# Chunk-selecting attention into a gMLP block: a new table of orders, engines and PSUM banks

## The chip, the cores and the metric

The kernel runs on one core of one Trainium2 chip. The metric is the device time of one execution in microseconds (us); the median of three runs stands for a kernel. In the text PE is TensorE, DVE VectorE, ACT ScalarE, POOL GpSimd and SP the queue of SyncE, which issues DMAs.

## The reference

The first half is attention over q, k and v of 4 batches, 8 heads, 768 rows and 64 columns, where each row of q looks only at 6 of the 24 chunks of 32 keys: those whose upper bound is highest. The second half is a gMLP block on the attention's output, with weights of 512 to 1024, a gating matrix over the 768 rows, and 512 to 512 back.

```
k_min, k_max = k_chunks.min(axis=3), k_chunks.max(axis=3)
ub = sum(maximum(q*k_min, q*k_max), axis=-1)          # 24 bounds for each row
ub = where(causal, ub, -1e9); top_chunks = argsort(ub)[..., -6:]
scores = where(in a top chunk and not in the future, q @ k.T / 8, -1e9)
x = softmax(scores) @ v                                # then heads side by side: 4 x 768 x 512
h = gelu_tanh(x @ w_in); u, v = h[..., :512], h[..., 512:]
v_n = (v - mean(v)) / sqrt(var(v) + 1e-6) * g_ln
out = x + (u * (w_sg @ v_n + b_sg)) @ w_out
```

## The kernel before

The work is cut into 16 pairs of heads (p = 0 to 15; four pairs make one batch) and 4 gMLP blocks (b = 0 to 3, one for each batch). For a pair, `kside` (L561) transposes the keys on PE ("ktr"), reduces each chunk to its minimum and maximum on DVE (L570, into `Wall`), and copies the transposed keys out of PSUM into `KA` ("kev", L364 or L367). From pair 10 on `kside_full` (L585) casts the keys ("kcast", into kbx or IND) and lets a DMA transpose them into `KA`. `qside` (L628) transposes the queries, copies them into `qT` ("qev"), makes their positive part `rT` ("rel"), and casts them into `QA` ("qcast"); `vside` casts the values into `vx` ("vcast"). `select` (pairs 0 to 3, L651) and `select_full` (two pairs at once, L704) compute the bounds on PE, transpose them on DVE into `U`, take the eight largest of each row with MAX8, compare (`Dn`) and transpose back (`Dt`). For pairs 4 to 15 `Dt` is then copied into rows of `QA` ("qd"), so that one matmul gives the score and its mask. `scores` and `scores_full` (L804, L768) run the score matmuls into the two PSC banks, ACT takes exponentials (L844, L795) into `E`, POOL clears the part in the future (L800, "aff"). `head` (L855) multiplies with the values ("pv", L867; "pvd", L874), DVE takes the reciprocal of the sum (L882, "rcp"), and the product goes into `XS` ("xs"): one DVE instruction for six tiles (L890), or six on ACT (L888).

When a batch is complete, `xtrans` brings `XS` transposed into `xT` (by PE and an eviction "xev" for block 0 and the last piece, else by DMA, "dt_x"), and `moe_h` (L912) runs its matmuls: "hv" (L921) with a GELU on ACT (L925), statistics on DVE, the normalised `vhat` (L944 on ACT, else on DVE, "vhat"), and "hu" (L961) with its GELU. `moe_g` (L970) multiplies with the gating matrix `wsgT` (L978), scales and gates on DVE (L984, L988), multiplies with w_out (L997), adds x (L1007) and stores (L1014, "st"). The last block's second half is stored in halves of 256 columns, out of `qn`. Early on the weights are cast to bf16 ("wic", "wsc", "woc"), w_sg is transposed by PE and evicted into `wsgT` ("wev"), and the masks `IND` and `INDF` are made ("ini", L410; "mrow" copies INDF into `KA`).

None of this is issued in the order of the program. `_build` (L259) only records operations with `Program.op` (L57): engine, function, a cost in ns, a tag, what is read and written. `TABLE` (L1093) says in which order each of the five queues issues them, which PSUM bank each of 328 tiles takes ("slots"), and for some movable operations which engine ("engine"); an operation that is not named there takes the first engine in its call of `flex` (L356) or `either` (L373). `place` (L101) adds the dependence of a PSUM tile on the one before it in its bank, `link` (L123) puts a wait wherever an operation depends on another queue, and `emit` writes the queues out. A queue issues strictly in its order, so an instruction that waits holds all behind it. The costs were used in the search that made the table; nothing at run time reads them.

`flex` is the helper through which nearly all copies, casts and relus go; its last lines choose the instruction:

```
        eng = ENG.get("_".join(str(x) for x in tag), first)

        def fn(e):
            if eng == "act":
                return e.activation(dst(), src(), ACTF.Relu if relu else ACTF.Copy)
            if relu:
                return e.tensor_scalar(dst(), src(), 0.0, None, op0=ALU.max)
            return e.tensor_copy(dst(), src())
```

So an ACT copy is L364, a relu on DVE or POOL is L366, a copy on these L367.

## Time and profile before

| | us |
|---|---|
| median of three runs (lowest, highest) | 214.52 (213.18, 215.04) |
| span of the profiled execution | 211.8 |
| the profiled execution's own time | not shown with the profile; the median is 2.7 above the span |
| busy: PE, DVE, ACT, POOL | 198.9, 182.5, 168.0, 125.5 |
| granted clock of TensorE | 1.00 of full speed in every stretch |

The span runs from the first instruction to the last. An engine's busy time counts its own instructions; PE's is modelled from pipelined matmuls, so that it can read a little high. The chain of waits follows the work that ended last back to the start. The stretches below are cut where the first hv matmul of blocks 0, 1 and 2 starts (42.2, 101.3 and 150.5) and at three points between and behind them.

### The profile page before, as it was taken

How to read it: one execution, taken by the hardware profiler on the slowest of the kernel's cores; microseconds unless marked ns; L12 is line 12 of the kernel's file. 1: busy time of each engine (PE TensorE's matmuls, PEld its weight loads, DVE VectorE, ACT ScalarE, POOL GpSimd, SP SyncE). 2: the span in 40 equal slices, each digit the busy share in tenths (PEclk: the TensorE clock that was granted, in tenths of full speed). 3: DMA queues.
4: the chain of work that ended last, by engine and by line, in shares of the span. 5: the costliest groups of instructions: out<-in, count | busy, mean ns of one | idle time of the engine just before them, and what ended most of it. 6: DMA issues, size and time to landing. Idle time of an engine off the chain costs nothing.

```text
span 211.8 us, 6001 instructions
## 1 busy us (share of the span) xinstructions
PE 198.9 (94%) x2347; PEld 128.0 (60%) x2363; DVE 182.5 (86%) x526; ACT 168.0 (79%) x271; POOL 125.5 (59%) x170
## 2 busy tenths in 40 slices
PE   7788999999999998989999989999999999999993
PEld 2556777845675676668356766676545767555641
DVE  3899899799999998889999997868977786687994
ACT  3678999999999999999779968999878979258000
POOL 7648997883849997969843977399370163011000
PEclk9999999999999999999999999999999999999999
DMA  7999999996399989998899386399990004301217
GB/s 152 219 220 231 232 256 324 335 292 125 92 213 272 216 156 235 190 180 148 176 256 203 65 196 120 87 235 168 216 233 0 3 3 138 88 0 56 92 50 248
DMA packets 99773, 35.58 MB, mean 168 GB/s; under 512 B 94497, under 2 KB 95265, under 8 KB 99746
## 3 DMA queue, kind: packets, MB, share of 16 engines
q1 hardware_dynamic: 99746, 35.21, 78.7%
q8 instruction: 18, 0.29, 0.6%
q14 instruction: 9, 0.07, 0.1%
HBM read 24.38 MB, written 6.29 MB: 145 GB/s over the span
## 4 chain that ended last, share of the span: by engine, by line
PE 59%; ACT 20%; DVE 14%; DMA 4%; issue 2%; SPq 0%; DVEq 0%
PE PSG L978 11%; ACT E L795 10%; PE PSC L789 9%; PE PSG L961 8%; PE PSG L997 8%; PE PSG L921 7%; PE PSG L867 5%; DVE Wall L570 4%; PE PSG L540 3%; ACT XS L888 3%; DMA KA<-kbx 2%; PE PSC L829 2%; PE PSG L874 2%; DMA kn<-in_k_dram 2%; DVE KA L367 1%
## 5 line engine op out<-in xcount | busy, mean ns | idle before, releaser
L795 ACT ACTIVATE E<-PSC 128x1024 bf16<-128x1024 f32 (+1 forms) x72 | 62.8, 925 | 3.4 <-PE PSC L789 2.8
L789 PE MATMUL PSC<-QA,KA 128*128 128x128 bf16 (+2 forms) x336 | 37.7, 247 | 2.3 <-ACT E L795 2.0
L978 PE MATMUL PSG<-wsgT,vhat 128*128 128x384 bf16 x192 | 35.1, 327 | 0.1
L789 PEld LDWEIGHTS PSC<-QA,KA 128*128 128x128 bf16 x336 | 24.0, 98 | 13.8 <-ACT E L795 6.0
L800 POOL TENSOR_SCALAR_AFFINE_SELECT E<-E 128x768 bf16<-128x768 bf16 x24 | 20.5, 861 | 19.3 <-ACT E L795 19.0
L978 PEld LDWEIGHTS PSG<-wsgT,vhat 128*128 128x128 bf16 x192 | 17.7, 98 | 11.5 <-ACT XS L888 0.6
L367 POOL CAST QA<-qT 64x768 bf16<-64x768 f32 (+1 forms) x27 | 22.2, 821 | 4.0 <-PE PSC L789 2.4
L961 PE MATMUL PSG<-xT,winb 128*128 128x384 bf16 x128 | 23.9, 327 | 0.0
L570 DVE TENSOR_REDUCE Wall<-PSG 128x12 f32<-128x384 f32 x40 | 20.5, 547 | 2.8 <-PE PSG L540 2.8
L844 ACT ACTIVATE E<-PSC 128x1024 bf16<-128x1024 f32 (+1 forms) x24 | 20.7, 924 | 2.8 <-PE PSC L835 2.6
L966 ACT ACTIVATE uT<-PSG 128x384 bf16<-128x384 f32 x32 | 15.3, 487 | 8.4 <-PE PSG L961 8.1
L997 PE MATMUL PSG<-woutb,uT 128*128 128x512 bf16 x85 | 21.3, 379 | 0.6
L921 PE MATMUL PSG<-winb,xT 128*128 128x512 bf16 x91 | 21.1, 380 | 0.7 <-issue 0.4
L984 DVE SCALAR_TENSOR_TENSOR PSG<-PSG,glnT,bsgbc 128x384 f32<-128x384 f32 x32 | 19.5, 613 | 2.2 <-PE PSG L978 2.0
L367 POOL COPY QA<-Dt 32x576 bf16<-32x576 bf16 x19 | 12.5, 659 | 13.9 <-DVE Dt L748 9.7
L867 PE MATMUL PSG<-vx,E 128*128 128x65 bf16 x480 | 19.9, 194 | 0.7 <-ACT XS L888 0.5
L925 ACT ACTIVATE vgb<-PSG 128x512 f32<-128x512 f32 x24 | 14.0, 596 | 8.1 <-PE PSG L921 8.1
L867 PEld LDWEIGHTS PSG<-vx,E 128*128 128x128 bf16 x480 | 17.3, 97 | 3.5 <-ACT XS L888 1.4
L988 DVE TENSOR_TENSOR uT<-PSG,uT 128x384 bf16<-128x384 f32 x32 | 17.7, 554 | 0.9 <-ACT uT L966 0.2
L930 DVE BATCH_NORM_STATS2 stats<-vgb 128x6 f32<-128x512 f32 x24 | 15.8, 682 | 1.6 <-ACT vgb L925 1.4
L1007 DVE TENSOR_TENSOR osb<-PSG,XS 128x512 f32<-128x512 f32 x21 | 14.2, 683 | 3.4 <-PE PSG L997 3.0
L961 PEld LDWEIGHTS PSG<-xT,winb 128*128 128x128 bf16 x128 | 11.6, 98 | 8.8 <-ACT uT L966 2.3
(121 smaller groups left out, 388.8 us busy)
## 6 DMA issues: line engine op xcount, KB each, us to landing
...
```

What stands on the lines that cost most here:

```text
L367: return e.tensor_copy(dst(), src())
L570: P.op("dve", lambda d, m=m, op=op, t=t, c0=c0, c1=c1: d.tensor_reduce(W[w][:, m, c0 // 32:c1 // 32], t.ap()[:, 0:c1 - c0].rearrange("p (c ...
L789: r = e.matmul(t.ap()[:, o:o + n], KA[w][i][:, 128 * kb:128 * kb + 128], QA[w][i][:, q0:q0 + n], start=True, stop=True)
L795: P.op("act", lambda e, t=t, c0=c0, c1=c1, i=i: e.activation(E[es][:, i, c0:c1], t.ap()[:, 0:c1 - c0], ACTF.Exp, scale=SCALE), act(c1 - c0 ...
L800: P.op("pool", lambda g, ev=ev: g.affine_select(ev, ev, pattern=[[0, NT], [1, 128]], compare_op=ALU.is_ge, fill=0.0, base=0, channel_multi ...
L844: P.op("act", lambda e, t=t, c0=c0, c1=c1, n=n: e.activation(E[es][:, :, c0:c1], t.ap().rearrange("p (i x) -> p i x", i=2)[:, :, 0:n], ACT ...
L867: r = e.matmul(t.ap()[:, 65 * qb:65 * qb + 65], E[es][:, i, a:a + 128], vx[w][:, kb, i, :], start=first, stop=False, skip_group_check=True)
L921: r = e.matmul(t.ap()[:, 0:F], xT[s][:, dk, 128 * qt:128 * qt + 128], winb[:, dk, F:DFF], start=(dk == 0), stop=(dk == NDK - 1))
L961: r = e.matmul(t.ap()[:, 0:TG], winb[:, dk, 128 * fb:128 * fb + 128], xT[s][:, dk, TG * tg:TG * tg + TG], start=(dk == 0), stop=(dk == NDK ...
L978: r = e.matmul(t.ap()[:, 0:TG], vhat[s][:, sb, 128 * fb:128 * fb + 128], wsgT[:, sb, TG * tg:TG * tg + TG], start=(sb == 0), stop=(sb == N ...
L984: P.op("dve", lambda d, t=t, fb=fb, tg=tg: d.scalar_tensor_tensor(t.ap()[:, 0:TG], t.ap()[:, 0:TG], glnT[:, fb:fb + 1], bsgbc[:, TG * tg:T ...
L997: r = e.matmul(t.ap()[:, 0:DM], gT[s][:, fb, 128 * qt:128 * qt + 128], woutb[:, fb, :], start=(fb == 0), stop=(fb == NF - 1))
```

## The change

The table is replaced as a whole, and the cost functions take other constants. Both programs have 1293 operations with the same tags and shapes. 114 of the 328 PSUM tiles take another bank. 70 operations change engine: 22 from ACT to DVE, 18 from POOL to ACT, 13 from DVE to ACT, 10 from ACT to POOL, 4 stores from SP to ACT, 2 from POOL to DVE, 1 from DVE to POOL:

- ACT to DVE: rel_0, kev_1_0, kev_2_1, wev_2, wev_5, kev_3_0, qev_4_0, qev_4_1, rel_4, xev_0_0, xev_0_1, qev_5_0, rel_5, vhat_0_1, vhat_1_1, vhat_3_5, xs_4_0, xs_5_0, xs_9_0, xs_9_1, qev_14_1, qev_15_0
- POOL to ACT: ini_0, ini_1, qcast_0, wic_2, wsc_3, mrow_0_1_0, mrow_2_0_0, rel_7, rel_8, rel_12, rel_13, qd_9_1, kcast_12_0, kcast_15_0, qcast_13_1, qcast_14_0, qcast_14_1, vcast_14
- DVE to ACT: rel_1, rel_14, qev_2_0, qev_2_1, qev_5_1, qev_11_1, wev_3, kev_4_0_1, kev_4_1_0, kev_4_1_1, xev_0_2, vhat_0_3, vhat_3_1
- ACT to POOL: ini_2, wic_0, wsc_2, wsc_4, woc_2, vcast_4, qd_12_1, qd_13_0, qd_15_1, kcast_15_1
- POOL to DVE: rel_2, rel_15; DVE to POOL: qd_15_0; SP to ACT: the stores st_3_1, st_3_3_0, st_3_4_0, st_3_5_256

The diff, cut: the head of the SP order, the head of the engine list, and of the cost functions one, with the two lines of `flex` that set costs and the mark of a port.

```diff
-def dve(n, over=70, rate=1.0):
+def dve(n, over=64, rate=1.0):
     o = n / rate / 0.96 + over
-    return o, o + 83
+    return o, o + 84
...
-    def flex(first, others, dst, src, n, tag, reads, writes, ps=(), relu=False, shift=False):
+    def flex(first, others, dst, src, n, tag, reads, writes, ps=(), relu=False, shift=False, half=False):
...
-                 port=eng == "pool" or (eng == "dve" and relu))
+                 port=not ps)
...
     "sp": (
-        "38 36 37 39 41 40 43 42 45 46 74 47 73 48 72 71 136 142 44 134 135 133 183 49 79 184 132 138 82 80 185 75 186 "
+        "37 36 39 38 40 41 42 43 45 46 47 72 73 48 71 74 142 44 134 136 135 138 133 49 79 132 184 75 183 77 242 243 80 "
...
     "engine": (
-        "ini_0:pool ini_1:pool kev_0_0:dve rel_0:act wic_0:act kev_2_0:dve qev_2_0:dve qev_2_1:dve rel_2:pool "
+        "qcast_0:act rel_1:act rel_3:act wic_2:act mrow_3_0_0:act mrow_2_0_0:act mrow_0_1_0:act wsc_3:act rel_6:act "
...
```

In the SP order 36 and 37 are the two key loads of pair 0, 38 and 39 its two query loads. Lines of the changed kernel are two higher than those of the kernel before (L366 there is L364 here).

DVE in the opening, from the end of pair 0's selection to the transposing of pair 1's, before (a number behind a name is the buffer: rT1 is the positive part of pair 1's queries, U1, m8_1, Dn1 and Dt1 its selection, KA2 the keys of pair 2):

```order
L700 STREAM_TRANSPOSE Dt0<-Dn0 128x288
L582 TENSOR_TENSOR Wall<-Wall 128x24
L410 TENSOR_TENSOR INDF<-IND 128x768
L366 TENSOR_SCALAR rT1<-qT1 128x576
L367 CAST KA2_0<-PSG0 128x384
L570 TENSOR_REDUCE Wall<-PSG0 128x12 x2
L683 STREAM_TRANSPOSE U1<-PSG1 128x288
L690 MAX m8_1<-U1 128x8 x9
L570 TENSOR_REDUCE Wall<-PSG0 128x12
L367 COPY qT2<-PSG1 128x384 x2
L696 TENSOR_TENSOR Dn1<-U1,m8_1 128x288
L700 STREAM_TRANSPOSE Dt1<-Dn1 128x288
```

and after the change, the rows that end with the same instruction:

```order
L369 CAST KA1_0<-PSG0 128x384
L572 TENSOR_REDUCE Wall<-PSG0 128x12
L572 TENSOR_REDUCE Wall<-PSG1 128x12
L685 STREAM_TRANSPOSE U1<-PSG1 128x288
L369 CAST KA2_0<-PSG0 128x384
L692 MAX m8_1<-U1 128x8 x9
L572 TENSOR_REDUCE Wall<-PSG0 128x12
L698 TENSOR_TENSOR Dn1<-U1,m8_1 128x288
L584 TENSOR_TENSOR Wall<-Wall 128x24
L368 TENSOR_SCALAR rT2<-qT2 128x576
L412 TENSOR_TENSOR INDF<-IND 128x768
L702 STREAM_TRANSPOSE Dt1<-Dn1 128x288
```

The relu of pair 1 and the two copies of pair 2's queries have left for ACT; the cast of pair 1's keys and the relu of pair 2 have come. The INDF sum has moved from the front of the piece to a place between Dn1 and Dt1.

ACT at pairs 6 and 7, the last exponentials ahead of pair 5's XS copies, before:

```order
L364 ACTIVATE KA0_1<-PSG0 64x384
L795 ACTIVATE E0<-PSC0 128x640
L364 ACTIVATE KA1_0<-PSG0 64x384
L364 ACTIVATE KA1_1<-PSG0 64x384
L795 ACTIVATE E0<-PSC1 128x1024
L795 ACTIVATE E1<-PSC0 128x1024
L888 ACTIVATE XS<-PSG1,rden0 128x64 x6
L795 ACTIVATE E1<-PSC1 128x1024
L795 ACTIVATE E0<-PSC0 128x1024
L888 ACTIVATE XS<-PSG1,rden1 128x64 x6
```

and after (XS of six tiles is one head's product on ACT):

```order
L366 ACTIVATE KA0_0<-PSG0 64x384
L797 ACTIVATE E0<-PSC1 128x640
L366 ACTIVATE KA1_0<-PSG0 64x384
L366 ACTIVATE KA0_1<-PSG0 64x384
L366 ACTIVATE KA1_1<-PSG0 64x384
L797 ACTIVATE E1<-PSC1 128x1024
L797 ACTIVATE E0<-PSC0 128x1024
L797 ACTIVATE E1<-PSC1 128x640
L890 ACTIVATE XS<-PSG1,rden1 128x64 x6
```

Of the two groups of XS copies one is left here; the other is an instruction of DVE now.

ACT while pairs 9 to 11 are scored, before:

```order
L364 ACTIVATE kbx0<-kn2 128x6x64
L795 ACTIVATE E0<-PSC1 128x1024
L795 ACTIVATE E0<-PSC0 128x640
L888 ACTIVATE XS<-PSG1,rden1 128x64 x6
L364 ACTIVATE QA3_0<-Dt3 32x576
L795 ACTIVATE E0<-PSC0 128x640
L795 ACTIVATE E0<-PSC1 128x1024
L888 ACTIVATE XS<-PSG1,rden0 128x64 x6
```

and after:

```order
L366 ACTIVATE rT1<-qT1 128x576
L366 ACTIVATE QA3_0<-Dt3 32x576
L797 ACTIVATE E0<-PSC1 128x1024
L366 ACTIVATE QA1_1<-qT1 64x768
L797 ACTIVATE E0<-PSC0 128x1024
L366 ACTIVATE QA2_1<-qT2 64x768
L797 ACTIVATE E0<-PSC1 128x640
L797 ACTIVATE E0<-PSC0 128x1024
L797 ACTIVATE E0<-PSC1 128x1024
L366 ACTIVATE QA2_0<-qT2 64x768
```

The kbx cast (it comes 16 rows further down now) and both groups of XS copies are gone from this piece; a relu (rT1) and three casts of queries (QA1, QA2) stand between the exponentials instead.

## Rows read from the trace of the kernel before

**Rows 1.** The page, parts 1 and 4: busy time by engine, and the chain by engine

```profile
PE 198.9 (94%) x2347; PEld 128.0 (60%) x2363; DVE 182.5 (86%) x526; ACT 168.0 (79%) x271; POOL 125.5 (59%) x170
...
PE 59%; ACT 20%; DVE 14%; DMA 4%; issue 2%; SPq 0%; DVEq 0%
```

**Rows 2.** Each engine's busy time by stretch (us from the span's start, length first)

```profile
core 0: us, PE busy (x) PEld busy (x) DVE busy (x) ACT busy (x) POOL busy (x), PEclk, DMA share, GB/s
0.00:42.20 42.20, 37.68 (x605) 26.15 (x605) 36.18 (x119) 33.76 (x49) 33.01 (x54) 1.00 1.10 246
42.20:78.30 36.10, 35.27 (x320) 22.63 (x322) 35.40 (x108) 34.61 (x59) 26.88 (x36) 1.00 0.93 202
78.30:101.30 23.00, 21.10 (x366) 15.26 (x366) 20.19 (x60) 22.68 (x47) 19.27 (x25) 1.00 1.04 177
101.30:120.90 19.60, 19.55 (x134) 11.45 (x131) 18.97 (x56) 17.07 (x27) 12.64 (x17) 1.00 0.99 185
120.90:150.50 29.60, 28.18 (x490) 19.85 (x491) 24.48 (x78) 26.40 (x44) 21.38 (x26) 1.00 0.81 153
150.50:181.90 31.40, 31.00 (x311) 19.08 (x314) 24.50 (x62) 24.43 (x33) 10.98 (x14) 1.00 0.45 106
```

**Rows 3.** The chain of waits in order of time: start, us, what

```profile
1.88 3.56 DMA kn<-in_k_dram
...
6.07 1.95 DVE Wall L570 x4
...
58.30 0.81 ACT vhat L944
...
69.55 0.73 ACT vx L364
...
79.33 1.24 ACT XS L888 x6
...
121.12 4.56 DMA KA<-kbx
```

**Rows 4.** The timeline of SP's queue (start, us; in brackets idle time and what ended it)

```profile
1.31 1.11 SPq L510 DMA_DIRECT2D kn<-in_k_dram  x2
```

**Rows 5.** The timeline of PE at the start

```profile
1.24 3.95 PE L385 MATMUL PSC<-vhat 128*128 128x512 bf16 x9 [1.24 <-DVE vhat L379]
...
5.49 0.87 PE L540 MATMUL PSG<-identF,kn 128*128 128x128 f32 x6 [0.30 <-DMA kn<-in_k_dram]
```

**Rows 6.** Groups by line and shape: xcount | busy us, mean ns of one | idle before

```profile
L367 DVE CAST KA<-PSG 128x384 bf16<-128x384 f32 x3 | 1.6, 550 | 0.0
...
L890 DVE TENSOR_TENSOR XS<-PSG,rden 128x384 bf16<-128x384 f32 x27 | 14.8, 554 | 0.7
...
L364 ACT ACTIVATE rT<-qT 128x576 f32<-128x576 f32 x6 | 4.1, 690 | 0.0
...
L364 ACT ACTIVATE qT<-PSG 128x384 f32<-128x384 f32 x26 | 12.3, 491 | 1.6 <-PE PSG L540 1.3
...
L944 ACT ACTIVATE vhat<-vgb,nmr,rstd 128x512 bf16<-128x512 f32 x7 | 5.6, 809 | 0.5 <-DVE nmr L938 0.4
...
L367 POOL CAST QA<-qT 64x768 bf16<-64x768 f32 x23 | 18.9, 821 | 3.8 <-PE PSC L789 2.4 <-DVE qT L367 0.6 <-ACT E L795 0.2
```

**Rows 7.** The timeline of ACT while pairs 8 to 13 are made

```profile
125.70 0.52 ACT L364 ACTIVATE kbx<-kn 128x384 bf16<-128x384 f32 x1 [1.12 <-DMA KA<-kbx]
...
128.72 1.34 ACT L888 ACTIVATE XS<-PSG,rden 128x64 bf16<-128x64 f32 x6 [0.99 <-DVE rden L882]
```

**Rows 8.** The timelines of SP and DVE at the end

```profile
206.95 2.83 SPq L1014 DMA_DIRECT2D out_dram<-qn  x6
...
206.50 2.48 DVE L1007 TENSOR_TENSOR qn<-PSG,XS 128x256 f32<-128x256 f32 x6
```

**Rows 9.** The timeline of DVE, the subtraction of L624 at two times

```profile
95.94 0.17 DVE L624 TENSOR_TENSOR Wall<-Wall 128x48 f32<-128x48 f32 x1
...
143.10 1.32 DVE L624 TENSOR_TENSOR Wall<-Wall 128x48 f32<-128x48 f32 x1
```

More of the change, by code (lines that the diff above doesn't have):

```diff
@@ L227, in _, with gps, pe, dmac @@
                 run("sp", eng)
-def dve(n, over=70, rate=1.0):
+def dve(n, over=64, rate=1.0):
     o = n / rate / 0.96 + over
-    return o, o + 83
+    return o, o + 84
 def act(n):
-    o = n / 1.2 + 67
-    return o, o + 100
-def gps(n, over=45, rate=1.0):
+    o = n / 1.2 + 56
+    return o, o + 112
+def gps(n, over=47, rate=1.0):
     o = n / rate + over
-    return o, o + 50
-def pe(*cols, over=3):
-    o = sum(max(c / 2.4 + 2.5, 29) for c in cols) + over
-    return o, o + 164 - over
+    return o, o + 46
+def pe(*cols, over=0):
+    o = sum(max(c / 2.4 + 2.5, 30) for c in cols) + over
+    return o, o + 164
 def pe32(*cols):
-    o = sum(c * 2 / 2.4 + 2.5 for c in cols) + 28
-    return o, o + 136
-def dmac(issue=530):
+    o = sum(c * 2 / 2.4 + 2.5 for c in cols)
+    return o, o + 165
+def dmac(issue=450):
     return issue, issue
@@ L354, in _build @@
     ENG = dict(x.split(":") for x in TABLE["engine"].split())
-    def flex(first, others, dst, src, n, tag, reads, writes, ps=(), relu=False, shift=False):
-        costs = {"act": (n / 1.2 + 52, n / 1.2 + 168), "pool": (2.85 * n, 2.85 * n + 50) if relu else (n + 12 + 145 * shift, n + 60 + 160 * shift),
-                 "dve": (n / 1.92 + 67, n / 1.92 + 150) if relu else (n / 0.96 + 64, n / 0.96 + 147)}
+    def flex(first, others, dst, src, n, tag, reads, writes, ps=(), relu=False, shift=False, half=False):
+        rate = 0.96 if ps and not half else 1.92 if ps or not half else 3.84
+        costs = {"act": (n / 1.2 + 54, n / 1.2 + 170) if ps else (n / 1.2 + (210 if shift else 94), n / 1.2 + 204),
+                 "pool": (2.78 * n, 2.78 * n + 48) if relu else (n + 8 + 130 * shift, n + 54 + 10 * shift),
+                 "dve": (n / rate + 66 + 106 * shift, n / rate + 150)}
         eng = ENG.get("_".join(str(x) for x in tag), first)
@@ L374, in either @@
         eng = ENG.get("_".join(str(x) for x in tag), first)
-        o = P.op(eng, fns[eng], costs[eng], tag, reads=reads, writes=writes, ps=ps, port=eng == "pool" or (eng == "dve" and port))
+        o = P.op(eng, fns[eng], costs[eng], tag, reads=reads, writes=writes, ps=ps, port=port)
         o.alts = {x: costs[x] for x in (first,) + others}
@@ L522, in load_rows @@
             bass.AP(src.tensor, 2 * p * S * DH, ap)), dmac(),
-             (nm, p), writes=[(nm, s, i) for i in range(2)], dma=f"{nm}{s}", xfer={1: 1780, 2: 1350, NT: 1100}[run], bulk=NBULK)
+             (nm, p), writes=[(nm, s, i) for i in range(2)], dma=f"{nm}{s}", xfer={1: (1780, 96), 2: (1350, 48), NT: (1100, 16)}[run], bulk=NBULK)
     def load_v(p):
```

86 lines of the change are left out of this document (43 added, 43 removed), and 117 rows, old and new, of the table TABLE.

## Prediction

> **What bounds the kernel now.** I read the page's busy shares and chain of waits first: PE is busy 94% of a span of 211.8 us, and the chain that ended last lies on PE for 59%, on ACT for 20%, on DVE for 14% and on DMA for 4% [rows 1]. An order can take nothing from PE's own work, so whatever a new order gains comes out of the other 40%, and a table of stretches is needed that says where these lie. I cut the span at the starts of the gMLP blocks [rows 2]. PE is busy 37.68 of 42.20 us in the opening, 35.27 of 36.10 and 21.10 of 23.00 around block 0, 19.55 of 19.60 behind it, 28.18 of 29.60 while pairs 8 to 13 are made, 31.00 of 31.40 in the next. So two of the six stretches are full of matmuls, and PE's idle time in the others is 4.52, 0.83, 1.90 and 1.42 us. DVE comes closest beside it from 42.20 to 78.30 (35.40 of 36.10), ACT from 78.30 to 101.30 (22.68 of 23.00).
>
> The chain of waits says the same in single steps [rows 3]. In the opening it runs over the key load and then over DVE (reductions over key chunks, transposes, casts). From 58.30 on it is on ACT: a vhat of 0.81, later a vcast of 0.73 (vx), then XS copies of 1.24 us. At 121.12 it waits 4.56 us for a transposing DMA that ACT's kbx copy needs.
>
> **The change, part by part.** No operation comes or goes; 70 of 1293 stand on another engine, and the rest is order and PSUM banks. The cost functions feed nothing that is issued: 0. I price the stretches one at a time, against the profiled execution. Its own total is not shown beside its span; the median of the runs, 214.5, is 2.7 above the span, and I take these 2.7 us as what lies around it.
>
> *Opening, 0 to 42.2.* Both key loads of pair 0 now stand ahead of its query loads. Before, the two key issues take 1.11 us from 1.31 [rows 4], behind one query issue; the key rows need 3.56 us to land [rows 3], and the first transposes start at 5.49 with 0.30 of idle time that this load ended, because the warm-up matmuls were over at 1.24 + 3.95 = 5.19 [rows 5]. One issue earlier the load is in before the warm-up ends: -0.3. Against that, ahead of pair 3's selection DVE takes on seven movable operations (kev_1_0, kev_2_1, kev_3_0, qev_4_0, qev_4_1, rel_0, rel_2) and gives up kev_4_0_1, qev_2_0, qev_2_1, rel_1. At 0.55 each (the DVE row of KA [rows 6], also for the relus) that is 3 more, +1.65. Sum +1.35 if all of it is on the path. DVE is busy 36.18 of 42.20 here [rows 2], so it has gaps; I take half, **+0.6**. Ends: -0.3, where the gaps take all of it, and +3.0, where two of the operations that read and write SBUF alone also wait for a POOL cast of 0.82 each [rows 6] (1.35 + 1.64).
>
> *Block 0, 42.2 to 101.3.* Between the first GELU of block 0 and the first of block 1 these leave ACT or move ahead of the stretch: rel_5 (0.69); wev_2, wev_5, vhat_0_1, wsc_2, wsc_4, vcast_4, woc_2 and mrow_3_0_0 (eight casts and copies, at the 0.81 of vhat); qev_6_0 (0.49); xs_4_0 and xs_5_0 (1.34 each, the XS rows of six [rows 7]). That is 0.69 + 6.48 + 0.49 + 2.68 = 10.34. To ACT come rel_7, rel_8, qd_9_1 (2.07 at 0.69), mrow_0_1_0, wsc_3, wev_3, vhat_0_3 (3.24) and qev_11_1 (0.49): 5.80. Net -4.5 us of ACT [rows 6]. DVE gets six of those that leave and loses three, +3 x 0.55 = +1.65, of which the two XS products cost it 0.554 each where ACT spent 1.34 [rows 6]. PE's idle time over this stretch is 0.83 + 1.90 = 2.73 [rows 2], and no more than that can go unless the new order also packs PE better. Some hand-over stays even where one engine is the bound: 0.32, as ACT itself idles from 78.30 to 101.30. So I take 2.73 - 0.32, **-2.4**. Ends: 0 (DVE, 0.70 from full in the first window, has no room for +1.65) and -4.5 (all of ACT's relief reaches the end, some of what counts as PE busy being slack, since busy matmuls are not PE at its peak).
>
> *101.3 to 120.9*: 0.05 us of PE idle, **0**. New PSUM banks could make PE wait for an eviction; its cover is the other bank with which a gMLP tile alternates, and without it one DVE eviction of 0.55 would show. Below nothing: the 0.05.
>
> *Pairs 8 to 13, 120.9 to 150.5.* ACT loses xs_9_0, xs_9_1, qd_12_1, qd_13_0, kcast_15_1, qev_14_1, qev_15_0, vhat_1_1 (2.68 + 1.38 + 0.52 + 0.98 + 0.81 = 6.37) and gets three relus, two key casts and three query casts (2.07 + 1.04 + 2.43 = 5.54; a few of either stand ahead of 120.9): -0.8. What counts more is that two of its waits go from where they stand: 1.12 ahead of the kbx copy, which moves behind a dozen more exponentials, and 0.99 ahead of XS copies that wait for a reciprocal on DVE and now are a DVE product [rows 7]. While ACT stands there, exponentials queue behind it, and PE's pv matmuls behind those. DVE has 5.12 idle in this stretch, so the XS product can wait there for free. PE's idle time of 1.42 is the cap; I take the 0.99 that the chain runs through, **-1.0**. Ends 0 and -1.4.
>
> *150.5 to 208.2*: PE full and its order almost the one before, **0** (0.40 of idle time is the most that could go).
>
> *Tail.* The last six stores leave SP from 206.95 for 2.83 us, 0.47 each, so the last is issued at 209.31; DVE's last product is done at 206.50 + 2.48 = 208.98 [rows 8]. Four of the block's stores now go from ACT, which has little left to do there, so the two queues issue beside each other: **-0.3** (0 to -0.3).
>
> Sum: 0.6 - 2.4 - 1.0 - 0.3 = -3.1. Span 208.7, time **211.4 us**.
>
> **A rule against it.** The new table puts more relus and key casts on DVE and others on POOL, and this kernel already shows the two in each other's way: the same 128x48 subtraction of L624 takes 0.17 us at 95.94 and 1.32 at 143.10 [rows 9]. The Trainium skill, "SBUF — State Buffer", section "SBUF: two separate sides", says that DVE and GpSimd share a port pair which is an exclusive lock: who starts first holds it for its whole instruction, and the other blocks. The two rows agree with it: the longer is 1.15 more, which is a length that POOL's instructions have here.
>
> **Rivals.**
> *Wider (A).* The relief of ACT reaches the end in full: opening 0, block 0 -4.5, pairs 8 to 13 -1.4, tail -0.3, together -6.2: 208.3. For it: the chain is on ACT at three operations that leave it, a vhat, a vcast and an XS copy [rows 3]. Against it: after every such step the chain goes back to PE or DVE, and DVE takes over part of the work.
> *Handed on (B).* What ACT loses becomes DVE's lateness: opening +1.35, block 0 -1.0, pairs 8 to 13 -0.5, tail -0.3, together -0.5: 214.0. For it: DVE at 35.40 of 36.10 [rows 2]. Against it: DVE's share is only +1.65 where ACT gives 4.5.
> *Slower (C).* In the opening DVE now also does the relu of pair 0, ahead of its selection, and between pair 1's Dn and its Dt stand the relu of pair 2 and the INDF sum, while POOL casts run on; two of the three meet one and wait 0.82 each, and selection is late by +3.0. Block 0 starts later by that much, DVE being nearly full there has nothing to give back (0), pairs 8 to 13 give -0.4, the tail -0.3: +2.3, 216.8. It decides once block 0's first matmul starts later than 42.2 by more than the 2.4 that block 0 is to give back. For it: the L624 rows [rows 9] and the chain on DVE from 6.07 [rows 3]. Against it: PE has exponentials and pv of pairs 0 to 2 to go on with, and DVE 6 us of gaps.
> By the lock rule C would be the likeliest if a POOL instruction ran at each of the three places. The order does not say that, and at 95.94 the subtraction met none.
>
> **How the numbers follow.** Forecast 0.45, A 0.17, B 0.22, C 0.16. The forecast's own range is 210.1 to 213.0 (the opening at -0.3 with pairs 8 to 13 at -1.4; or a third of block 0's term). A tenth or so of the forecast's chance lies above 212.4, and A all below it: faster by over 1% (2.1 us, about what a measurement of this kernel tells from none) 0.58. B and the rest of the forecast lie within 1%: 0.27. C lies beyond 216.7, nearly whole: 0.15. The range for 8 in 10 leaves out about half of A and most of C: 208.4 to 215.6.
>
> **What would show it.** Right: the first transposes at about 5.2; block 0's first hv matmul between 42 and 44; ACT's busy time from there to block 1's first hv matmul down by about 4 us, and the stretch down by 2 to 3 us; no XS copies ahead of pv in pairs 9 on ACT; last store issued within 0.2 us of DVE's last product. Wrong: a first hv matmul later than 44.6 (C); a shorter ACT with a chain now on DVE at the same length (B); a stretch from block 1's hv to block 2's that is longer than the 49.2 of before, which would mean that the new banks or the work brought to ACT cost what I put at 0.

## The result: slower by 1.3%, and the profile after

Four runs of the changed kernel have a median of 217.55 us (216.89 to 217.76), four of the kernel before beside them 214.78 (213.18 to 215.25): a ratio of 1.0133, with a 95% interval of 1.009 to 1.0176. Slower, where 211.4 and faster was forecast. Some executions of a kernel run longer than its others, and the ratios here and below leave these out. The profiled execution took 217.44 with a span of 215.5, 3.7 more than before; by the medians the difference is 2.8, so the profiled execution of before was among its quicker ones. From the page of the changed kernel, parts 1 and 4 (beside [rows 1]):

```profile
PE 198.2 (92%) x2347; PEld 129.1 (60%) x2363; DVE 185.2 (86%) x536; ACT 168.1 (78%) x250; POOL 113.6 (53%) x161
...
PE 62%; DVE 17%; DMA 10%; issue 3%; ACT 3%; SPq 2%; POOL 1%; DVEq 0%
```

PE has 0.7 us less to do and the span is 3.7 longer, so PE's idle time grew by 4.4. ACT left the chain (20% to 3%), as the change promises, and DMA came onto it (4% to 10%). Where the idle time lies shows when both spans are cut at the same instructions: the first hv matmul of block 0, its last w_out matmul, the first hv of block 1, its first gating matmul, the first hv of block 2, and the eighth w_out matmul from the end of the kernel (a matmul's start is that of its weight load). Busy times by stretch, the kernel before (its first stretch is that of [rows 2]):

```profile
42.20:99.10 56.90, 54.22 (x642) 37.01 (x647) 53.39 (x164) 55.09 (x102) 44.14 (x57) 1.00 0.98 194
99.10:101.30 2.20, 2.15 (x39) 0.88 (x38) 2.20 (x4) 2.19 (x4) 2.01 (x5) 1.00 0.78 152
101.30:113.20 11.90, 11.85 (x75) 6.09 (x72) 11.59 (x44) 9.40 (x17) 6.52 (x9) 1.00 1.20 211
113.20:150.50 37.30, 35.88 (x548) 25.21 (x551) 31.86 (x90) 34.07 (x54) 27.50 (x33) 1.00 0.78 151
150.50:206.10 55.60, 55.05 (x441) 31.89 (x447) 44.67 (x104) 33.49 (x50) 12.30 (x15) 1.00 0.30 77
206.10:211.80 5.70, 2.09 (x10) 0.77 (x8) 2.62 (x7) 0.00 (x0) 0.00 (x0) 1.00 0.71 246
```

and the changed kernel (columns as in [rows 2]: length, then PE, PEld, DVE, ACT, POOL):

```profile
0.00:43.50 43.50, 37.60 (x604) 26.45 (x605) 37.51 (x123) 35.13 (x50) 28.82 (x48) 1.00 1.11 240
43.50:98.50 55.00, 53.01 (x632) 35.95 (x637) 52.80 (x165) 51.74 (x87) 40.55 (x58) 1.00 0.92 194
98.50:102.70 4.20, 2.76 (x21) 1.71 (x21) 2.45 (x4) 4.18 (x7) 3.71 (x5) 1.00 1.24 190
102.70:117.00 14.30, 13.39 (x107) 7.59 (x108) 13.43 (x46) 11.88 (x22) 7.15 (x9) 1.00 1.12 193
117.00:153.20 36.20, 33.51 (x528) 24.05 (x533) 31.93 (x100) 31.95 (x39) 20.83 (x28) 1.00 0.82 154
153.20:210.10 56.90, 55.81 (x450) 32.56 (x456) 44.44 (x95) 33.25 (x49) 12.51 (x15) 1.00 0.26 68
210.10:215.50 5.40, 2.11 (x10) 0.78 (x8) 2.64 (x7) 0.00 (x0) 0.00 (x0) 1.00 0.75 261
```

By stretch the lengths differ by +1.3, -1.9, +2.0, +2.4, -1.1, +1.3 and -0.3. These lengths also hold matmuls that the new order has moved from one stretch to another, so PE's idle time says more: in the opening 4.5 us before and 5.9 after, from block 0's first hv to block 1's 2.7 and 3.4, from there to block 2's 1.5 and 3.6, and behind that 4.2 and 4.4. Block 0 is 1.9 shorter up to its last w_out matmul, of which 1.2 are matmuls that went elsewhere and 0.7 is idle time; the few us from there to the start of block 1 lost 2.0, 1.4 of it idle. PE's timeline shows what it stood for (in brackets the idle time and what ended it):

```profile
41.54 0.51 PE L908 MATMUL PSG<-identB,XS 128*128 128x128 bf16 x6 [0.62 <-ACT qT L366]
...
102.72 1.90 PE L923 MATMUL PSG<-winb,xT 128*128 128x512 bf16 x8 [1.27 <-DVE osb L1009]
...
117.00 2.11 PE L980 MATMUL PSG<-wsgT,vhat 128*128 128x384 bf16 x12 [0.73 <-DVE vhat L951]
...
153.43 0.81 PE L923 MATMUL PSG<-winb,xT 128*128 128x512 bf16 x3 [2.49 <-issue]
```

All four stand at the start of a gMLP block, just ahead of it, or at its gating; for blocks 1 and 2 the kernel before has no more than 0.38 in these places. At 41.54 the eviction is late because ACT's queue stands at a cast of w_in for its load:

```profile
40.05 1.06 ACT L366 ACTIVATE winb<-vgb 128x1024 bf16<-128x1024 f32 x1 [0.76 <-DMA vgb<-in_moe_w_in_dram]
```

For 102.72 and 153.43, DVE's timeline says why:

```profile
100.25 1.84 DVE L591 TRANSPOSE_TENSOR_REDUCE Bn<-kn 128x24 f32<-128x768 f32 x2 [1.83 <-DMA kn<-in_k_dram]
102.01 0.65 DVE L1009 TENSOR_TENSOR osb<-PSG,XS 128x512 f32<-128x512 f32 x1
102.59 3.54 DVE L591 TRANSPOSE_TENSOR_REDUCE Bn<-kn 128x24 f32<-128x768 f32 x4
...
106.41 1.24 DVE L932 BATCH_NORM_STATS2 stats<-vgb 128x6 f32<-128x512 f32 x2
...
146.18 0.20 DVE L884 RECIPROCAL rden<-PSG 128x6 f32<-128x6 f32 x1 [1.75 <-PE PSG L876]
...
147.10 0.56 DVE L892 TENSOR_TENSOR XS<-PSG,rden 128x384 bf16<-128x384 f32 x1
```

DVE stands 1.83 for a key load and does two key reductions (Bn) before the last sum of block 0 (osb), whose PSUM bank block 1's first hv takes. Four more reductions stand ahead of block 1's statistics. The reductions are only in part new: before, three stood ahead of that sum (98.27 to 100.96) and one behind it, and none waited for its load. At 146.18 DVE waits 1.75 for pair 11's first head, while its second head is done, and only then makes the XS that block 2's x is transposed from. SP's timeline:

```profile
92.31 2.36 SPq L900 DMA_TRANSPOSE xT<-XS  x1
94.71 0.57 SPq L522 DMA_DIRECT2D kn<-in_k_dram  x1
...
143.81 2.11 SPq L900 DMA_TRANSPOSE xT<-XS  x1
145.97 1.29 SPq L598 DMA_TRANSPOSE KA<-IND  x1
147.30 1.29 SPq L598 DMA_TRANSPOSE KA<-kbx  x1
148.64 2.17 SPq L900 DMA_TRANSPOSE xT<-XS  x1
```

and SP at the same place in the kernel before, the x transposes ahead of the key transpose that follows:

```profile
142.53 4.38 SPq L898 DMA_TRANSPOSE xT<-XS  x3
146.95 2.20 SPq L596 DMA_TRANSPOSE KA<-kbx  x1
```

The late key load is issued at 94.71, behind a transposing DMA that waits for XS. Two key transposes of 1.29 stand ahead of the last x transpose of block 2, which leaves at 148.64 and lands 4.5 later, at 153.12; PE's first weight load of hv follows at 153.18. So the gap of 2.49, for which the profile names no releaser, ends with this landing.

One wait of PE inside block 0 is of rival B's kind: 0.69 at 88.73 for a subtraction on DVE (L584), which with the one beside it took 0.87 from 87.71, while POOL's cast of the values ran from 87.68 for 0.87. The kernel before has no wait for this subtraction.

The tail went as forecast: DVE ends at 210.52 + 2.48 = 213.00, SP's last issue at 211.31 + 1.73 = 213.04, and ACT's, which has three of the last six stores, at 213.38:

```profile
210.52 2.48 DVE L1009 TENSOR_TENSOR qn<-PSG,XS 128x256 f32<-128x256 f32 x6
```

```profile
211.31 1.73 SPq L1016 DMA_DIRECT2D out_dram<-qn  x3
```

### The profile page after: what moved, and what is told of

The parts are those of the page before. It is cut to its first block, busy times and chain, and to the rows that moved or that the text cites. A ratio compares the mean times of both kernels' runs of the same rounds, so it can differ in the third digit from the quotient of the medians.

```text
span 215.5 us, 5962 instructions
## 1 busy us (share of the span) xinstructions
PE 198.2 (92%) x2347; PEld 129.1 (60%) x2363; DVE 185.2 (86%) x536; ACT 168.1 (78%) x250; POOL 113.6 (53%) x161
## 4 chain that ended last, share of the span: by engine, by line
PE 62%; DVE 17%; DMA 10%; issue 3%; ACT 3%; SPq 2%; POOL 1%; DVEq 0%
PE PSG L980 15%; PE PSC L791 9%; PE PSG L999 8%; DMA kn<-in_k_dram 7%; PE PSG L542 5%; PE PSG L963 5%; PE PSG L923 4%; PE PSG L869 4%; DMA vgb<-in_moe_w_in_dram 4%; DVE stats L932 4%; DVE Bn L591 3%; PE PSG L722 3%; DVE vhat L951 2%; PE PSG L675 2%; PE PSC L831 2%
## 5 line engine op out<-in xcount | busy, mean ns | idle before, releaser
L791 PE MATMUL PSC<-QA,KA 128*128 128x128 bf16 (+2 forms) x336 | 36.7, 246 | 0.0
L369 POOL COPY QA<-Dt 32x576 bf16<-32x576 bf16 x22 | 15.0, 680 | 21.8 <-DVE Dt L750 20.8
L923 PE MATMUL PSG<-winb,xT 128*128 128x512 bf16 x91 | 21.8, 379 | 4.3 <-issue 2.7
L369 POOL CAST QA<-qT 64x768 bf16<-64x768 f32 (+1 forms) x23 | 19.2, 835 | 10.9 <-ACT qT L366 7.3
L572 DVE TENSOR_REDUCE Wall<-PSG 128x12 f32<-128x384 f32 x40 | 21.1, 545 | 2.8 <-PE PSG L542 2.6
L892 DVE TENSOR_TENSOR XS<-PSG,rden 128x384 bf16<-128x384 f32 x31 | 17.1, 553 | 0.7
```

Of the source, the lines that this page charges most:

```text
L572: P.op("dve", lambda d, m=m, op=op, t=t, c0=c0, c1=c1: d.tensor_reduce(W[w][:, m, c0 // 32:c1 // 32], t.ap()[:, 0:c1 - c0].rearrange("p (c ...
L791: r = e.matmul(t.ap()[:, o:o + n], KA[w][i][:, 128 * kb:128 * kb + 128], QA[w][i][:, q0:q0 + n], start=True, stop=True)
L923: r = e.matmul(t.ap()[:, 0:F], xT[s][:, dk, 128 * qt:128 * qt + 128], winb[:, dk, F:DFF], start=(dk == 0), stop=(dk == NDK - 1))
```

## The experiments

The theory: the new order makes new waits at the starts of blocks, by what stands ahead in SP's and DVE's queues. The rivals: C (DVE's added work of the opening, or its port), and a loss spread over the new engines and banks. Every edit moves entries of the order table; in the diffs they are written by tag (kn: key load of a pair, qn: query load, wi: w_in load, kT: key transpose by DMA, kred: key reduction), "+" where an entry now stands and "-" where it stood. Kernels named a_ start from the changed kernel, those named b_ from the one before; ratios are to the kernel before, with the 95% interval.

### One move on SP at a time

```diff
 a_kn13 (SP)
+kn_13
 kn_14 qn_11_1 dt_x_1_1
-kn_13
 a_xt2 (SP)
+dt_x_2_3
 kT_15_0 kT_14_0
-dt_x_2_3
 a_win (SP)
+wi_2 wi_3
 qn_6_0 qn_6_1
-wi_2
 qn_5_0
-wi_3
 a_three: all of these
```

> The changed kernel with one load moved: on SP the key load of pair 13 stands ahead of that of pair 14 and of the second DMA transpose of x for block 1. Theory W (the loss is made of waits at the starts of the gMLP blocks, each from one queue's order): in the changed kernel this load is ready to be issued at 87.73 (its buffer is free) but leaves at 94.71, lands at 100.23, and DVE, which stands in front of kred_13_1, holds os_0_5 and with it PE's first hv of block 1. Issued some 6 us earlier, DVE's wait of 1.83 goes, hv of block 1 starts 1.2 to 1.8 earlier, and since the stretch behind it has little PE idle time the end comes 1.0 to 1.8 earlier: 215.8 to 216.5. Rival S (slack: the wait is covered, another takes its place at once): under 0.4, 217.1 or more. Rival C (the loss comes from the opening): 0.

1.012 (1.0071 to 1.017). DVE's wait is gone:

```profile
99.06 1.83 DVE L591 TRANSPOSE_TENSOR_REDUCE Bn<-kn 128x24 f32<-128x768 f32 x2
100.81 0.65 DVE L1009 TENSOR_TENSOR osb<-PSG,XS 128x512 f32<-128x512 f32 x1
```

The first hv of block 1 starts at 101.98 and not 102.72, though block 0 began 0.4 later here. So the wait is what the trace says; its 1.1 us can't be told from nothing in the time, which was forecast at 215.8 to 216.5 and has a median of 218.24 (see the last section on TensorE's clock).

> The changed kernel with one DMA transpose moved: on SP the last x transpose of block 2 stands ahead of the key transposes kT_15_0 and kT_14_0. Theory W: it is issued at about 147.7 where it left at 148.64, and has no transposes queued ahead of it in the DMA engines either, so PE's gap of 2.49 ahead of hv_2_0 shrinks by 1.0 to 1.6 and the end comes as much earlier: 215.9 to 216.6. What is left of the gap (about 1) belongs to pair 11's XS, done at 147.66 where it was 145.19. Rival S: the two key transposes that are now late hold pairs 14 and 15, under 0.4. Rival C: 0.

1.0091 (1.0055 to 1.0126), which can't be told from the 1.0133 of the changed kernel. The gap ahead of block 2 halves and does not go (a_xt2, PE):

```profile
153.36 0.81 PE L923 MATMUL PSG<-winb,xT 128*128 128x512 bf16 x3 [1.29 <-issue]
```

> The changed kernel with two loads moved: on SP the third and fourth row blocks of w_in stand ahead of the queries of pairs 5 and 6. Theory W: in the changed kernel the fourth lands at 42.07, is cast until 43.16, and hv of block 0 starts at 43.51 (42.21 before). Two to three loads earlier it lands at 39 to 40, and hv starts at 42.0 to 42.6, 0.9 to 1.5 earlier. Block 0 is then bound by ACT and DVE as before, so half or more can be lost again by block 1: the end 0.3 to 1.3 earlier, 216.2 to 217.2. Rival C (selection in the opening is late by DVE and POOL): hv of block 0 starts no earlier, 0.

1.0321 (1.0275 to 1.0367), a miss. The w_in load lands no earlier (the last piece at 42.0, 42.1 in the changed kernel), for it leaves SP only 0.6 earlier (33.99) and the DMA engines are full here (a share of 1.11 in the changed kernel's opening), and the query load behind it is late (a_win, PE):

```profile
43.42 0.52 PE L542 MATMUL PSG<-identF,qn 128*128 128x128 f32 x3 [4.03 <-DMA qn<-in_q_dram]
```

The first hv of block 0 moves from 43.5 to 48.9. PE's queue needs pair 6's queries ahead of hv, so a load can't be moved alone.

> The changed kernel with all three moves on SP: key load of pair 13, last x transpose of block 2, and w_in. Theory W: the waits are in different stretches and add up: 1.0 to 1.8, 1.0 to 1.6 and 0.3 to 1.3, together 2.3 to 4.5 earlier, 213.0 to 215.2, so that the time is that of the kernel before or less. Rival S: under 1.2, 216.3 or more. Rival C: 0.

1.0172 (1.0101 to 1.0243, from two of six executions; the median of all six is 221.48): much the same hole in the opening, 3.89, so it says nothing of the other two.

### The opening and rival C

```diff
 a_open: a_win, and
 (PE)
-qtr_6_0
 ... qtr_5_1 hv_0_1 qtr_6_1
+qtr_6_0
 (ACT)
-qev_6_0
 ... qev_5_1 gv_0_1
+qev_6_0
 a_fix3: a_open, a_kn13 and a_xt2
 a_fix4: a_fix3, and (DVE)
-kred_14_1 os_0_5 kred_14_0
+os_0_5 ... dt_10 kred_14_1 kred_14_0
 a_relu: rel_0 from DVE to ACT (behind qev_0_0),
         rel_2 from DVE to POOL (behind aff_0_0)
```

> The changed kernel with w_in and one query transpose put in another order: on SP the third and fourth row blocks of w_in ahead of the queries of pairs 5 and 6, and with it PE's transpose of pair 6's first query half (qtr_6_0) and ACT's eviction of it behind the first hv of block 0. Theory Q (what cost a_win its 4.2 us was PE's order: PE stands in front of qtr_6_0 until that load lands, with all of block 0 behind it, and the clock falls after the idle time): with the transpose out of the way the gap of 4.03 goes, the clock stays at 1.00, w_in's last block lands near 41.0 and hv of block 0 starts at 42.2 to 43.0 where it is 43.5 in the changed kernel: 0.5 to 1.3 earlier, of which half or more reaches the end: 216.2 to 217.3. Rival D (the DMA engines are full until 45, so any reorder only shifts the landing of something that is needed): hv at 43.5 or later, no gain, 217.5 or more.

1.0278 (1.0227 to 1.0329): with the queries moved behind hv, PE stands 2.00 for pair 5's query load, and 1.35 for pair 6's eviction. First hv at 44.5, not earlier.

> The moves of a_open and those of a_kn13 and a_xt2 together. Theory W with Q: the three stretches add up, 0.5 to 1.3, 1.1 and 1.0 (as the spans of a_kn13 and a_xt2 at an undisturbed clock stand to those of the changed kernel): 2.3 to 3.4 earlier, 214.1 to 215.3, the time of the kernel before. Rival S: each gain is taken by the next wait, 216.5 or more.

1.0179 (1.0125 to 1.0233), far from the forecast time of the kernel before; its opening has the same wait for pair 5's query load, 2.19.

> a_fix3 with one more move: on DVE the key reductions kred_14_1 and kred_14_0, which the new order has ahead of block 1's statistics, go behind the selection of pairs 10 and 11 (as before). Theory W: DVE has 1.9 us less to do ahead of bns_1, whose rstd is 4.0 later than before in the changed kernel, so PE's gap of 0.73 ahead of pt_1 goes and hv_1's of os_0_5 too: 0.7 to 1.5 more than a_fix3, 212.8 to 214.4, at or below the kernel before. Rival: PE has other work to do in that time, so only the 0.73 can go at most, and pairs 14 and 15 are late in turn: no better than a_fix3.

1.0288 (1.0243 to 1.0333): the reductions pushed behind the statistics take the 0.73 ahead of block 1's gating down to 0.16, and make PE stand 1.58 ahead of its second group of gating matmuls. They had to be somewhere; DVE has no free place near. Both runs carry the worse opening, so they don't judge the theory.

> The changed kernel with two relus put back to engines off DVE: rel_0 to ACT behind qev_0_0, rel_2 to POOL. Rival C of the prediction (these relus wait for POOL's port on DVE and make selection late): pair 1's Dt comes 0.5 to 1.6 earlier than at 18.78, hv of block 0 1 to 3 earlier, and the end 1 to 3 earlier, 214.6 to 216.6. Theory W: Dt of pairs 0 to 3 is within 0.5 of the kernel before already, so nothing is to be had: 217.1 to 218.0, or later where a relu of 1.7 on POOL holds what stands behind it.

1.0078 (1.004 to 1.0116). The time lies where rival C put it, but not by C's mechanism: pair 1's Dt starts at 18.70 where it started at 18.78, and block 0 no earlier. The two relus of the opening hold up nothing on DVE, and one costs more on POOL (a_relu, PE):

```profile
20.34 0.69 PE L675 MATMUL PSG<-qT,Wall 64*32 64x288 f32 x8 [1.55 <-POOL rT L368]
```

Pair 2's selection ends 1.9 later (its Dt starts at 27.15 against 25.27). The first hv is at 44.05, which is no difference: in the eight traces that have the changed kernel's opening as it is (the changed kernel, a_kn13, a_xt2, a_dve and the four with a_x11 in their names) it starts between 43.5 and 44.6, and in the four of the kernel before and its variants between 41.8 and 42.2. In the changed kernel itself the places that C named show no wait; by line, duration in ns (lowest, median, highest):

```profile
L368 DVE TENSOR_SCALAR rT<-qT x5: 453/459/770, 8.1 to 142.3; 128x576 f32<-128x576 f32 x5
...
L412 DVE TENSOR_TENSOR INDF<-IND x1: 553/553/553, 18.3 to 18.3; 128x768 bf16<-128x768 bf16 x1
```

So C's mechanism is not what costs the time. Where this run gained what it did stays open: block 1 starts 1.3 earlier (101.43) than in the changed kernel's trace, from a later block 0.

### Block 2's x, and the relief of before alone

```diff
 a_open2: (SP)
+qn_5_1 qn_6_0 qn_6_1   (were ahead of wi_2)
 (PE) qtr_6_0 behind hv_0_0, in bank 1; (ACT) qev_6_0 behind gv_0_1
 a_x11q: a_xt2, and (DVE)
+rcp_11_1 xs_11_1
 rcp_11_0 xs_11_0
-rcp_11_1 xs_11_1
 a_x11pe: (PE)
+pvd_11_0
 sc_12_1_0
-pvd_11_0
 (POOL)
+aff_11_0
 qd_12_0 qd_13_1 aff_11_1 qd_12_1 qd_13_0 qcast_15_0
-aff_11_0
 a_x11: a_x11q and a_x11pe
 a_x11k: a_x11 and a_kn13
 a_dve: a_x11q without its SP move
 a_best: a_x11k and a_open2, with kred_14_1 behind gt_1_1_3
         and kred_14_0 ahead of kred_15_1
```

> The changed kernel with pair 6's query loads put behind pair 5's on SP (the rest of the queue as it was) and PE's transpose and ACT's eviction of their first half behind the first hv of block 0, in another bank. Theory D (the DMA engines are full until 45: what counts is which loads PE's order needs first; the changed kernel has pair 6's queries ahead of half of w_in and of pair 5's): now nothing that PE needs ahead of hv is late, w_in lands at 40.3 to 41.2 and hv of block 0 starts at 42.0 to 43.0, against 43.5 in the changed kernel and 44.5 in a_open. The gaps that the two moves of a_open made (2.00 and 1.35) are gone, the clock stays at 1.00, and the end comes 0.5 to 1.3 earlier than the changed kernel: 216.2 to 217.1. Rival: the opening has no better order with these engines: hv at 43.4 or later and 217.4 or more.

1.0067 (1.0027 to 1.0106). First hv at 43.17, earlier than in any of those eight traces, with a new gap of 1.59 ahead of pair 7's key transposes; block 1 at 102.71, as in the changed kernel. Its start doesn't hang on the opening: ahead of the last sum of block 0 DVE stands 0.26 for the key load and, here, 0.80 for a store that still reads that sum's buffer.

> The changed kernel with pair 11's head drawn together: POOL's aff_11_0 ahead of the four copies of pairs 12 and 13's selection (two of which the change brought from ACT to POOL), PE's pvd_11_0 ahead of a score tile, DVE's XS of head 11_1 ahead of 11_0's, and on SP the last x transpose of block 2 ahead of two key transposes. Theory X (PE runs dry at 150.9 because XS of pair 11 is 2.0 later than before, and from there to hv_2 it takes 5.5 of DMA): XS of pair 11 is done at 146.0 to 146.9 instead of 147.66, x lands at 150.8 to 151.9, the gap of 2.49 falls to 0.3 to 1.2, and the end comes 1.2 to 2.1 earlier: 215.4 to 216.4. Rival (PE's own lateness of 1.3 at that place decides, or DMA's): the gap stays above 1.8 and the end within 0.6.

0.9975 (0.994 to 1.0011): the loss is gone.

> The other half of a_x11: the changed kernel with DVE's XS of head 11_1 ahead of 11_0's, and on SP the last x transpose of block 2 ahead of two key transposes; POOL and PE as changed. Theory X1: DVE used to wait 1.75 for pvd_11_0 with 11_1's XS ready behind it; XS of the pair is done 0.7 earlier and x leaves 0.3 earlier still, the gap of 2.49 falls to 1.0 to 1.6: 216.0 to 216.8. Rival (the transposing DMA's 4.5 to 5.5 is what decides, and its length hangs on what is queued ahead of it): the key transposes being behind it, x lands 2 earlier and the gap is under 0.6: 215.0 to 215.6.

1.0021 (0.9993 to 1.0048). The gap ahead of block 2's first hv is gone in a_x11q:

```profile
150.92 0.81 PE L923 MATMUL PSG<-winb,xT 128*128 128x512 bf16 x3
```

and both x transposes leave ahead of the key's (SP):

```profile
143.96 4.17 SPq L900 DMA_TRANSPOSE xT<-XS  x2
148.18 1.29 SPq L598 DMA_TRANSPOSE KA<-IND  x1
```

> Half of a_x11: the changed kernel with POOL's aff_11_0 ahead of the copies of pairs 12 and 13's selection and PE's pvd_11_0 ahead of a score tile; DVE's and SP's order as changed. Theory X1 (the lateness is in the head's own work, POOL and PE): the XS of pair 11 is done 0.4 to 0.7 earlier and no more, since DVE still makes 11_0 ahead of 11_1: 0.3 to 0.8 of a_x11's 2.7: 216.4 to 217.1. Theory X2 (any microsecond off the chain from XS to x counts once, and the gap decides also whether the clock falls): as X1 for the gap, and fewer executions with a mean clock below 0.995.

1.0103 (1.0058 to 1.0149), the gap still 1.78: the earlier product of the first head is of little use while the last transpose leaves at 148.14. Theory X2's fewer executions at a lower clock didn't come: the mean clock is below 0.995 in seven of ten.

> The changed kernel with two entries moved on DVE alone: reciprocal and XS of head 11_1 ahead of 11_0's. a_x11q, which had this and one entry of SP, came to 1.002 of the kernel before, and the SP entry alone (a_xt2) to 1.009. Theory X1 (the order of two heads on DVE is the larger part): XS of the pair is done 0.7 earlier, but the x transpose stays behind the two key transposes on SP, which leave at 147.3 to 148.6, so it leaves no earlier than 148.6: the gap stays at 2.0 to 2.5 and the ratio at 1.010 to 1.014. Only both together free the chain. Rival (DVE alone is enough): 1.003 to 1.007.

1.0138 (1.0083 to 1.0193), with 2.05 (a_dve, PE):

```profile
153.44 0.38 PE L923 MATMUL PSG<-winb,xT 128*128 128x512 bf16 x1 [2.05 <-issue]
```

XS is made earlier, and its transpose still leaves at 148.66, behind the key transposes. Of the gap of 2.49, DVE's order alone takes 0.4, SP's alone 1.2, both together all of it, in one trace each (a_relu, which leaves this place alone, has 2.72, and a_kn13 2.08, so the 0.4 is within what executions differ by); in the time, only both together show.

> a_x11 and the key load of pair 13 ahead of pair 14's (a_kn13). Theory W: a_x11 stands level with the kernel before (ratio 0.9975); DVE's wait for that load is another 1.1 ahead of block 1, so 0.990 to 0.995 of the kernel before, 213.0 to 214.3, faster than both. Rival S: the 1.1 are waited for at block 2, 0.996 or more.

0.9994 (0.9966 to 1.0022). Its stretches (ends: first hv of blocks 0, 1 and 2, eighth w_out matmul from the end):

```profile
0.00:43.70 43.70, 38.03 (x604) 26.61 (x605) 37.59 (x123) 35.10 (x50) 28.41 (x48) 1.00 1.09 241
43.70:101.60 57.90, 55.60 (x652) 37.68 (x656) 54.92 (x169) 54.42 (x91) 43.88 (x61) 1.00 0.89 192
101.60:149.40 47.80, 46.55 (x635) 31.42 (x639) 43.43 (x130) 42.82 (x61) 28.27 (x37) 1.00 0.88 172
149.40:206.30 56.90, 56.00 (x457) 32.55 (x459) 45.64 (x112) 35.49 (x52) 12.47 (x15) 1.00 0.32 75
```

Against the kernel before: +1.5, -1.2 (of 59.1), -1.4 (of 49.2), +1.3. Theory W's 0.990 to 0.995 was missed: beside a_x11's 0.9975 the key load's 1.1 don't show. Nor is the forecast gain of blocks 0 and 1 there with the new waits out: the last two differences are nearly the same matmuls, which stand behind block 2's start instead of ahead of it (PE is busy 1.2 less in the one stretch and 0.95 more in the other), and PE's idle time in the two middle stretches is 2.3 and 1.25, where before it was 2.7 and 1.5.

> All repairs together: a_open2, a_x11, the key load of pair 13 early (a_kn13), and the two key reductions of pair 14 behind block 1's gating (kred_14_1 behind gt_1_1_3, kred_14_0 ahead of kred_15_1). Theory W: 0.5 to 1.3, 1.2 to 2.1, 1.1, and 0.5 to 1.0 for DVE being free ahead of block 1's statistics: 3.3 to 5.5 earlier than 217.5, 212.0 to 214.2, at or under the kernel before (214.8). Rival S: what is gained in one stretch is waited for in the next; above 215.5.

1.004 (1.0006 to 1.0073), not the time of the kernel before or less that theory W had: the regrouped opening brings new gaps, 1.55 ahead of pair 7's key transposes and 1.44 ahead of pair 11's query transposes.

```diff
 b_xs:   xs_4_0, xs_5_0, xs_9_0, xs_9_1 from ACT to DVE, each behind its rcp
 b_late: (PE)
-pvd_11_0
 pvd_11_1 sc_13_1_2 sc_12_1_0 ub_14
+pvd_11_0
 b_kbx:  (ACT)
-kcast_14_0
 ... exp_11_0_2 qev_15_0 exp_11_1_2 exp_11_1_1
+kcast_14_0
```

> The kernel before with one part of the change alone: the XS products of heads 4_0, 5_0, 9_0 and 9_1 are made on DVE, right behind their reciprocals, instead of by six instructions on ACT each; the order is otherwise that of before. Theory of the forecast's block 0 and pairs 8 to 13 (ACT's relief is worth time): PE's gaps ahead of pv_4_1, sc_7_1_0 and sc_10_0_0 (0.54, 0.96, 0.69) shrink, DVE has 0.55 for each, and the end comes 0.5 to 1.8 earlier than before: 213.0 to 214.3. Rival H (the relief is handed on: DVE is as full, and each XS ahead of other DVE work makes that late): within 0.4 of the kernel before or above.

0.9978 (0.994 to 1.0017). PE's waits of 0.54 for such a product and 0.96 for an exponential behind others are gone, and one of 1.50 has come, for a subtraction on DVE (b_xs, DVE, then POOL):

```profile
84.42 0.56 DVE L890 TENSOR_TENSOR XS<-PSG,rden 128x384 bf16<-128x384 f32 x1
84.89 2.21 DVE L582 TENSOR_TENSOR Wall<-Wall 128x24 f32<-128x24 f32 x2
```

```profile
84.50 0.82 POOL L367 CAST QA<-qT 64x768 bf16<-64x768 f32 x1 [0.82 <-PE PSC L789]
85.28 1.69 POOL L800 TENSOR_SCALAR_AFFINE_SELECT E<-E 128x768 bf16<-128x768 bf16 x2
```

In the kernel before this subtraction ran at 84.64, just ahead of POOL's cast, and the two took 0.24. Here it meets POOL and ends with it, at 87.1 and 87.0. The relief was handed on, as rival B says; the time shows no gain and no loss.

> The kernel before with one piece of the loss put in: PE's last six matmuls of head 11_0 (pvd_11_0) stand behind the bounds of pairs 14 and 15 instead of ahead of them, so that XS of pair 11 is done some 1.6 to 2.2 later (at 147.3 to 147.9 where it was 145.66), as late as in the changed kernel; nothing else is moved. Theory X: x lands as much later, PE's gap ahead of hv_2 grows from 0.38 to 1.6 to 2.5, in some executions the clock falls behind it, and the time is 1.2 to 3.0 above the kernel before: 216.2 to 218.0. Rival (the place is covered in the kernel before, and the loss comes from the new order as a whole): within 0.6 of it.

0.9991 (0.9965 to 1.0017): the pair's XS is done 1.8 later and block 2 starts only 0.4 later; in the order of before this lateness is absorbed. So late XS alone is not the loss; in this order no key transpose stands ahead of the x transpose.

> The kernel before with one piece of the change alone: ACT's kbx copy for pair 14 stands ten exponentials later, past the landing of the DMA that it waited 1.12 for. Forecast's term for pairs 8 to 13: PE's gap of 0.69 ahead of sc_10_0_0 goes, block 2's first hv starts 0.5 to 1.0 earlier if x is there by then: 0.3 to 1.0 under the kernel before, 0.995 to 0.999. Rival (x's transpose sets hv_2 anyway, 0.38 of gap there before): the gap moves to hv_2 and nothing is gained, 0.999 to 1.001.

0.9939 (0.9892 to 0.9986), 213.09 beside 214.57: 0.6% better than the kernel before, a little more than expected. PE's wait in the kernel before

```profile
127.19 0.62 PE L789 MATMUL PSC<-QA,KA 128*128 128x128 bf16 x7 [0.69 <-ACT E L795]
```

is gone in b_kbx, and ACT's exponentials run where it stood 1.12 for the kbx copy [rows 7]:

```profile
126.25 0.62 PE L789 MATMUL PSC<-QA,KA 128*128 128x128 bf16 x7
```

```profile
124.77 1.62 ACT L795 ACTIVATE E<-PSC 128x1024 bf16<-128x1024 f32 x2 [0.38 <-PE PSC L789]
```

## Why the prediction was wrong

The sum was -3.1 and came out +3.7 in the spans (+2.8 in the medians). Term by term, with the stretches of the prediction:

- **Opening, +0.6: measured +1.3**, within its ends; over the eight and four traces named above it is 1.3 to 2.8, so the changed kernel's own trace has the least of it. Right: the first transposes at 5.01, without the 0.30 of idle [rows 5]. The reason given, DVE's seven operations, found no support: with two of them elsewhere (a_relu) the start came no earlier. PE stands 0.62 for an eviction on ACT that is queued behind a cast of w_in waiting for its load, and the last piece of w_in lands at 42.07 where it landed at 40.95. So the order of loads is the likely cause; three orders tried made the start no better than 43.1, which doesn't show it, and how much of the 1.3 reaches the end stays open. Not all: a_x11q, whose block 0 starts at 44.5, takes the time of the kernel before.
- **Block 0, -2.4: measured +0.1** (59.1 to 59.2). The 2.4 were to come out of PE's idle time of 2.73, and that rose to 3.43. Up to the last w_out matmul 0.7 of it went. ACT lost only 1.4 busy us from hv to hv (57.3 to 55.9) and not 4.5: the list of moved operations left out what the new order brings in or takes out without a change of engine. At the end of the stretch DVE's wait for the key load, ahead of the last sum, gave 1.4 of idle time back. a_kn13 takes 1.1 of that out again in the trace.
- **101.3 to 150.5, 0 and -1.0: measured +1.3**. The waits that were to go went: in pairs 8 to 13 the gap of 0.69 is gone, and without it the kernel before gains 0.6% (b_kbx), so this term's mechanism was right. But idle time rose from 1.5 to 3.6: 2.49 ahead of block 2, for its late x, and 0.73 ahead of block 1's gating, for statistics that stand behind the key reductions. With x mended (a_x11k) idle time is 1.25 and the stretch 47.8, though most of the 1.4 that it is shorter than before are matmuls moved behind it.
- **150.5 to 208.2, 0: measured +1.3**, and 56.9 still in a_x11k. PE's busy time in it is 0.8 higher (55.05 to 55.81), so most of it is matmuls that now stand behind block 2's start; the rest is idle time. All of it lies ahead of block 3's first hv, and from there on both kernels take the same. It wasn't tried.
- **Tail, -0.3: measured -0.3.**

**The step that failed** is the "cap", by which PE's idle time of before bounded the terms from block 0 on: -2.4 out of 2.73, **0** for "0.05 us of PE idle", -1.0 with ends 0 and -1.4 for pairs 8 to 13. New waits were put at nothing. Idle time of before bounds what can be won, not what can be lost: a table that is replaced as a whole can set any wait ahead of a block's first matmul. What came in its place is idle time of 3.43 where 2.73 stood and 3.60 where 1.47 stood, most of all the 2.49 ahead of block 2's first hv, in the very stretch whose term was -1.0; with that gap undone (a_x11q) the ratio falls from 1.0133 to 1.0021. The one price given for a loss, 0.55 for a late eviction, was too small: the waits that came are of another kind (a load and a transpose behind others on SP). Beside it, ACT's relief in block 0 was put at 4.5 and measured 1.4. The prediction itself had named the sign: a stretch from block 1's hv to block 2's above 49.2. It is 50.5. The reason it gave there, the new banks or ACT's new work, is not what the traces show.

Of the rivals, C has the right sign and the wrong cause: the relus that it named did not wait, and the start of block 0 is not what decided. B's hand-over is real and is shown in b_xs, where the relief of ACT alone comes back as a wait on DVE, of 2.21 us where 0.24 stood, while POOL works. The Trainium skill, "SBUF — State Buffer", section "SBUF: two separate sides", says that a DVE instruction with two SBUF inputs and a GpSimd one that reads SBUF take a shared port pair as an exclusive lock, for one whole instruction. The trace agrees that DVE is blocked, and goes further: it stood through the rest of a cast and two selects. The rows that the prediction set beside the rule [rows 9] read otherwise than it read them, too: at 143.10 POOL's timeline shows the rest of a cast and a select (to 144.37), not one instruction of 1.15, and at 95.94 the subtraction did meet one, the last 0.1 of a select that ended at 96.05. The part of the loss that is shown by undoing it is block 2's x: a_x11q takes 1.0133 to 1.0021, and neither of its halves does. What the rest of the new order costs and gains was not taken apart; it comes to about nothing (0.9975 to 1.0021 with x mended and the opening as it is).
